# Six steps of an attention kernel form their own numerators by features, in four column tiles, and turn them back by DMA

## The chip, the cores and the metric

The kernel runs on one core of a Trainium2 chip. Its time is the device time of one execution, in microseconds (us), and the median over a few runs is what is compared. One further execution was recorded by the hardware profiler; its span (first to last instruction) and its own time are given below. The engines are PE (matrix products; PEld is its weight load), DVE (vector), ACT (scalar, exponentials), POOL (GpSimd) and SP (which here only issues DMAs).

## What is computed

Two attention layers over the same 2048 tokens of width 640 (32 heads of 20 features), mixed by a gate. Layer A is linear attention with softmax feature maps. Layer B, where the change lies, goes over the tokens in four segments of 512. Within a segment it is causal softmax attention, between segments a memory is carried:

```python
for s in range(4):                      # segments of L = 512 tokens
    p = softmax(qs @ ks.T * scale + mask)           # per head, causal
    a_dot = p @ vs                                  # "own" numerators over their denominators
    num, den = phi(qs) @ M, phi(qs) @ z + 1e-6      # the memory of earlier segments
    o = g * num / den + (1 - g) * a_dot
    M, z = M + phi(ks).T @ vs, z + phi(ks).sum(...)
return gate * A(x) + (1 - gate) * (concat(o) @ wo)
```

## The kernel before, in words

The first 126 us prepare weights, run layer A and the projections of B's first segment. From about 126.9 us on B's attention runs; the program is written out by hand there, engine by engine, in the order in which the Python code emits it.

**Steps and double steps.** A step is one segment and one group of four heads, so there are 4 x 8 = 32 (`Step`, L735); step k belongs to segment k // 8. Two steps a and b make a double step, of which there are 16, numbered 0 to 15. A double step has five bursts (`bursts`, L771). A burst (`emit_burst`, L751) writes scores of four heads into two PSUM tiles `st_ps` (L757, four row groups of PE, one for each head), ACT takes the exponential of each tile into `PT` (L761, 128 x 1024, key tokens on the partitions and query tokens along the columns), and POOL zeroes the triangles of the diagonal blocks (L768). The two tiles come from two pools of one buffer each, so PE can write a tile of the next burst only when ACT has read the one before.

**Own numerators.** `pv_items` (L805) makes, for each 128-query block j and head i, a sum over the key blocks c <= j: the weights are a 128 x 128 block of `PT`, the moving operand is `vB`, 20 value features and a column of ones, so that the denominator comes as column 21. That is 4 x (1 + 2 + 3 + 4) = 40 matmuls of 21 columns for a step (L811), with query tokens on the PSUM partitions. They go to bank 0 of `nda`, of which there is one. `mem_items` (L815) adds four matmuls with the memory (L819) and, except in the last segment, four that add to it (L824), in bank 1.

**Epilogue.** `emit_epi` (L831): DVE takes the reciprocal of both kinds of denominators (L836), multiplies it by the gates (L838) and both kinds of numerators by that (L848); POOL adds the two into `oB` (L851). For segments before the last, DVE and POOL also update the memory (L854, L857, L858).

**Fillers.** Between the bursts PE does dense work from a list: `h`, half projections for the next segment (L943), `o` and `f`, halves of output rows (L887; `f` of an early chunk is ten matmuls of 320 columns, otherwise five). All of it uses `proj` PSUM tiles, two buffers in all, and DVE moves each result out (L949, L898, L896). `t` issues on SP the DMA transpose of an `oB` chunk (`emit_oT`, L860, at L862), `u` the last four such (L981). SP is one queue and also carries the row outputs (L900).

**The order.** For each double step `PLAN` (L971) is a string: `A` and `D` are the first and last part of the own numerators of step a, with `D` also the memory's; `B` and `C` the same for the step b of the double step before; the other letters are fillers and feature work. Every item has a planned price, and `SHARES` (L976) says what part of the sum of prices is emitted before each of the five bursts.

Of the kernel before, what the change touches and what calls it, by code (L numbers as in the profile page):

```python
# [15 lines left out]
def kernel(  # L16
# [16 lines left out]
    P = 128  # L33
# [421 lines left out]
    kv_stack.close()  # L455
    a3_stack = ExitStack()
    resB = ctx.enter_context(tc.tile_pool(name="resB", bufs=1))
    vBs = [resB.tile([P, 4, H, DH + 1], BF16, name=f"vB{n}") for n in range(2)]
    a3e = a3_stack.enter_context(tc.tile_pool(name="a3e", bufs=KC, side="right", reuse_waits="tile"))
    a3w = a3_stack.enter_context(tc.tile_pool(name="a3w", bufs=2, side="right", reuse_waits="tile"))  # L460
    for W, src in ((WkB, B_wk), (WqB, B_wq)):
# [107 lines left out]
    def emit_zsum():  # L569
        emit_zz(emit_z(z_den[:, 0]))  # L570
        open_stages()
        for vB in vBs:
            nc.gpsimd.memset(vB[:, :, :, DH:DH + 1], 1.0)

    def emit_first_den():
        for n in range(NB):
# [130 lines left out]
    with ExitStack() as bctx:  # L707
# [24 lines left out]

        GP = 4 * (DH + 1)

        class Step:  # L735
            def __init__(self, k):
                self.s, self.g = divmod(k, G)
                self.PT = {}
                self.last = k == NSEG * G - 1
                self.nda = nda  # L740
                if self.g == 0:
                    oBs[self.s] = bw.tile([P, 4, D], BF16, name="oB")
                    og = Eqf[:, 2 * G * L + 2 * L + (self.s % 2) * L:2 * G * L + 2 * L + (self.s % 2 + 1) * L]
                    og = og.bitcast(F32).rearrange("p (n j h) -> p n j h", n=2, j=4)
                    om = omgS[:, 4 * self.s:4 * self.s + 4, None].to_broadcast([P, 4, H])
                    nc.gpsimd.tensor_tensor(out=og[:, 0], in0=om, in1=omgh_b[:, None, :].to_broadcast([P, 4, H]),
                                            op=ALU.mult)
                    nc.gpsimd.tensor_copy(out=og[:, 1], in_=om)
                    ogs[self.s] = og
# [55 lines left out]
        def pv_items(st, js):  # L805
# [6 lines left out]
                                     rhs=vB[:, c, 4 * st.g + i, :], start=(c == 0), stop=(c == j))  # L812
            return [(0.026 * (j + 1), lambda j=j, i=i: piece(j, i)) for j in js for i in range(4)]

        def mem_items(st):  # L815
            g = st.g

            def am(j):
                nc.tensor.matmul(st.nda[:, 1, j * GP:(j + 1) * GP], lhsT=phiq_block(st.s, g, j),  # L819
                                 rhs=Mbd[:, g].rearrange("p i e -> p (i e)"), start=True, stop=True)  # L820

            def mz(c):
                Mz = st.nda[:, 1, 4 * GP:5 * GP].rearrange("p (i e) -> p i e", i=4)
                nc.tensor.matmul(Mz, lhsT=phiks[st.s % 2][:, c, 4 * g:4 * g + 4, :],  # L824
                                 rhs=vBs[st.s % 2][:, c, 4 * g:4 * g + 4, :],
                                 start=(c == 0), stop=(c == 3))
            return ([(0.037, lambda j=j: am(j)) for j in range(4) if st.s > 0]
                    + [(0.037, lambda c=c: mz(c)) for c in range(4) if st.s < NSEG - 1]
                    + [(0.0, lambda: emit_epi(st))])

        def emit_epi(st):  # L831
            s, g = st.s, st.g
            n = 2 if s > 0 else 1
            ndv = st.nda[:, 0:n, 0:4 * GP].rearrange("p n (ji e) -> p n ji e", e=DH + 1)
            rec = bw.tile([P, 2, 16], F32, name="rec")
            nc.vector.reciprocal(out=rec[:, 0:n], in_=ndv[:, :, :, DH])  # L836
            recv = rec[:, 0:n].rearrange("p n (j i) -> p n j i", j=4)
            nc.vector.tensor_tensor(out=recv, in0=recv,  # L838
                                    in1=ogs[s][:, 0:n, :, 4 * g:4 * g + 4],
                                    op=ALU.mult)  # L840
            rb = rec[:, 0:n, :, None].to_broadcast([P, n, 16, DH])
            oview = oBs[s][:, :, g * 80:(g + 1) * 80].rearrange("p j (i d) -> p j i d", d=DH)
            if n == 1:
                nc.vector.tensor_tensor(out=oview, in0=ndv[:, 0, :, 0:DH].rearrange("p (j i) d -> p j i d", j=4),
                                        in1=rb[:, 0].rearrange("p (j i) d -> p j i d", j=4), op=ALU.mult)
            else:
                td = bw.tile([P, 2, 16, DH], F32, name="td")
                nc.vector.tensor_tensor(out=td, in0=ndv[:, :, :, 0:DH], in1=rb, op=ALU.mult)  # L848
                tdv = td.rearrange("p n (j i) d -> p n j i d", j=4)
                eng = nc.vector if s == NSEG - 1 and g == G - 2 else nc.gpsimd  # L850
                eng.tensor_tensor(out=oview, in0=tdv[:, 0], in1=tdv[:, 1], op=ALU.add)  # L851
            if s < NSEG - 1:
# [81 lines left out]
        def run_first(fns):  # L934
            if fns:
                fns.pop(0)()

        def half_item(part, sc, half):
            W = {"k": WkB, "q": WqB, "v": WvB}[part]
            hs = slice(half * 16, (half + 1) * 16)  # L940

            def mm(ps, k):
                nc.tensor.matmul(ps, lhsT=xq[:, sc // 4, k, sc % 4 * P:(sc % 4 + 1) * P],  # L943
                                 rhs=W[:, k, half * 320:(half + 1) * 320],
                                 start=(k == 0), stop=(k == KC - 1))
# [22 lines left out]

        PLAN = ("qhhhyzhokxooAD", "qhhByhChkzoxAooD", "qhhByhChkzxoAooD",  # L971
                "ooBqoyokCozxoADo", "hkhBhhChhqhyAhDztt", "khhBxhhqChfhyzAD",
                "khhBxhhqCfyzADt", "khhBxhhqChfyhzAD", "khhxtBhhqChyhADzt",
                "hhBhhqChfyhzAD", "hhBhhqCfhyzAthD", "hhBhhqhCftyhzAD",
                "fBftCfftAD", "ffBtCfftAD", "fBtfCffADf", "fBCuffAffD")
        SHARES = [[0.2, 0.42, 0.55, 0.78], [0.19, 0.4, 0.6, 0.84], [0.2, 0.4, 0.6, 0.81], [0.19, 0.38, 0.59, 0.78], [0.19, 0.38, 0.58, 0.81], [0.18, 0.41, 0.65, 0.86], [0.2, 0.4, 0.6, 0.83], [0.19, 0.4, 0.6, 0.83], [0.2, 0.4, 0.6, 0.8], [0.22, 0.39, 0.6, 0.82], [0.19, 0.39, 0.61, 0.82], [0.2, 0.39, 0.6, 0.82], [0.2, 0.4, 0.6, 0.8], [0.21, 0.4, 0.61, 0.8], [0.19, 0.37, 0.59, 0.82], [0.2, 0.41, 0.6, 0.84]]  # L976

        oT4 = oTA[:, 0:4]

# [7 lines left out]
        for dstep in range(NSEG * G // 2):  # L987
# [5 lines left out]
            for w in PLAN[dstep]:  # L993
                if w in "hfo":
                    items += {"h": halves, "f": fins, "o": aouts}[w].pop(0)
                elif w in "xy":
                    items.append((0.0, lambda part="kq"[w == "y"]: run_first(sums[part])))
                elif w in "kq":
                    items.append((0.0, lambda part=w: run_first(waiting[part])))
                elif w == "z":  # L1000
                    items.append((0.0, lambda: run_first(q_turns)))
                elif w == "u":
                    items += [(0.0, lambda n=n: turn_last(n)) for n in range(4)]
                elif w == "t":
                    items.append((0.0, lambda ch=turns.pop(0): emit_oT(ch)))
                else:
                    st = a if w in "AD" else prev
                    items += pv_items(st, (0, 1, 2)) if w in "AB" else pv_items(st, (3,)) + mem_items(st)
            whole = sum(w for w, _ in items)
            done = 0.0  # L1010
            for n, burst in enumerate(bursts(a, b)):
# [159 lines left out]
```

## Time and profile before

| | us |
|---|---|
| median of 3 runs | 316.44 (316.29 to 316.65) |
| the profiled execution, its own time | 315.58 |
| its span, first to last instruction | 313.6 |
| first exponential of double step 0 | 126.88 |
| first exponential of double steps 11, 12, 13, 14, 15 | 248.13, 259.41, 270.80, 281.16, 291.96 |
| end of the last exponential | 302.89 |

So 2.0 us of the execution lie outside the span, and the profiled execution is 0.86 us faster than the median. The first exponential of a double step is the tenth, twentieth and so on of the 160 instructions of L761 in the trace; their distance is used below as the length of a double step: 11.28, 11.39, 10.36, 10.80 and 10.93 us for 11 to 15.

In a row of the profile's timeline stand the start, the time from the first to the last instruction of a group, the engine, line, operation, operands, count and, in brackets, the idle time before it. PE rows overlap, since a matmul's recorded end lies behind the start of the next: what a group costs PE is the distance from its start to the next group's start.

### The profile page before, as it was taken

Reading aid. Unit: us, or ns where it says so; the run is one execution under the profiler, and the core shown is the slowest. Engines: PE = TensorE matmul, PEld = TensorE weight load, DVE = VectorE, ACT = ScalarE, POOL = GpSimd, SP = SyncE. Lnnn points to the kernel's source line nnn. Section 1 sums busy time; section 2 is a strip of 40 time slices with the busy share of each in tenths; the row PEclk is TensorE's granted clock in tenths of the full one; section 3 lists DMA queues with packets and bytes.
Section 4 is the critical chain, followed back from the end, with each engine's and each line's share of the span. In section 5 each row is a group of like instructions: output and inputs, shape, how many; then the busy total and the mean of one; then the engine's idle time right before and its main releaser. Section 6 shows DMA issues by size and latency. Waiting matters only on the chain.

```text
span 313.6 us, 10096 instructions
## 1 busy us (share of the span) xinstructions
PE 303.6 (97%) x4182; PEld 208.4 (66%) x4182; DVE 224.0 (71%) x508; ACT 252.0 (80%) x320; POOL 206.8 (66%) x308
## 2 busy tenths in 40 slices
PE   8999999999999999999999999999999999999995
PEld 7788877755578778465666666565666666565673
DVE  3477997999779997677758588777755765455553
ACT  4677888267846648999998999999998898998953
POOL 8588599103247989955657577688786877666550
PEclk9999999999999999999999999999999999999999
DMA  7989944439217998775421394473745545222132
GB/s 216 199 184 204 210 108 129 127 89 365 74 36 106 130 136 147 135 100 99 55 50 36 69 127 86 59 120 69 110 84 78 86 100 72 64 78 53 48 90 84
DMA packets 94007, 34.56 MB, mean 110 GB/s; under 512 B 82442, under 2 KB 93834, under 8 KB 93962
## 3 DMA queue, kind: packets, MB, share of 16 engines
q1 hardware_dynamic: 93386, 33.28, 54.4%
q10 hardware_dynamic: 576, 0.66, 0.7%
q8 instruction: 32, 0.52, 0.7%
q14 instruction: 13, 0.11, 0.1%
HBM read 6.10 MB, written 2.62 MB: 28 GB/s over the span
## 4 chain that ended last, share of the span: by engine, by line
PE 69%; ACT 19%; DVE 4%; POOL 3%; issue 2%; DMA 1%; ACTq 0%; DVEq 0%; POOLq 0%
ACT PT L761 16%; PE proj L943 10%; PE st_ps L757 10%; PE proj L887 9%; PE pk L242 7%; PE pq L420 7%; PE nda L811 7%; PE pv L242 7%; PE proj L557 3%; PE num L478 2%; PE kv_ps L393 2%; DVE tt L527 1%; DMA oTA<-oA 1%; POOL oA L686 1%; DVE rr L503 1%
## 5 line engine op out<-in xcount | busy, mean ns | idle before, releaser
L761 ACT ACTIVATE PT<-st_ps 128x1024 bf16<-128x1024 f32 x160 | 153.9, 1023 | 12.2 <-PE st_ps L757 9.8
L768 POOL TENSOR_SCALAR_AFFINE_SELECT PT<-PT 128x512 bf16<-128x512 bf16 (+1 forms) x130 | 84.4, 668 | 46.7 <-ACT PT L761 46.3
L811 PEld LDWEIGHTS <-PT 128*128 128x128 bf16 x1280 | 40.0, 96 | 9.0 <-issue 5.4
L811 PE MATMUL nda<-vB,PT 128*128 128x21 bf16 x1240 | 41.5, 173 | 0.1
L261 POOL TENSOR_TENSOR EkSn<-Ek,krec 128x1280 bf16<-128x1280 bf16 x15 | 35.1, 2360 | 9.2 <-DVE krec L260 7.3
L943 PEld LDWEIGHTS <-xTf 128*128 128x128 bf16 x300 | 26.5, 97 | 13.8 <-issue 5.3
L949 DVE CAST Z<-proj 128x320 bf16<-128x320 f32 x44 | 21.1, 488 | 16.7 <-PE proj L943 15.6
L427 ACT ACTIVATE Eq<-pq 128x1024 bf16<-128x1024 f32 x20 | 19.4, 1021 | 12.2 <-PE pq L420 12.2
L257 DVE TENSOR_REDUCE ksum<-Ek 128x64 f32<-128x1280 bf16 x16 | 23.6, 1474 | 7.2 <-ACT Ek L253 7.2
L527 DVE TENSOR_TENSOR tt<-num,rr 128x640 f32<-128x640 f32 x32 | 25.0, 812 | 4.6 <-POOL rr L520 1.8
L686 POOL TENSOR_TENSOR oA<-tt 128x640 bf16<-128x640 f32 x16 | 24.6, 1545 | 5.3 <-DVE tt L527 5.0
L887 PE MATMUL proj<-WkA,oTA 128*128 128x320 bf16 x160 | 28.0, 300 | 0.0
L757 PE MATMUL st_ps<-Z 32*128 32x512 bf16 (+3 forms) x256 | 24.9, 299 | 3.0 <-ACT PT L761 2.5
L253 ACT ACTIVATE Ek<-pk 128x640 bf16<-128x640 f32 x32 | 20.8, 703 | 7.9 <-PE pk L242 6.8
L757 PE MATMUL st_ps<-Eq 32*128 32x512 bf16 (+3 forms) x256 | 25.2, 299 | 1.5 <-ACT PT L761 1.2
L242 PEld LDWEIGHTS <-xTf 128*128 128x128 bf16 x200 | 22.6, 113 | 4.7
L851 POOL TENSOR_TENSOR oB<-td 128x320 bf16<-128x320 f32 x22 | 19.6, 889 | 4.4 <-DVE td L848 3.6
L420 PE MATMUL pq<-xTf,WqA 128*128 128x512 bf16 x100 | 22.4, 379 | 0.0
L887 PE MATMUL proj<-WvA,oT 128*128 128x320 bf16 x120 | 21.3, 300 | 0.0
L848 DVE TENSOR_TENSOR td<-nda,rec 128x640 f32<-128x640 f32 x23 | 19.0, 825 | 2.5 <-DVE rec L838 0.5
L836 DVE RECIPROCAL rec<-nda 128x32 f32<-128x32 f32 (+1 forms) x31 | 10.3, 331 | 12.8 <-PE nda L824 8.1
L887 PEld LDWEIGHTS <-oTA 128*128 128x128 bf16 x160 | 13.6, 97 | 8.3 <-issue 4.2
(183 smaller groups left out, 558.8 us busy)
## 6 DMA issues: line engine op xcount, KB each, us to landing
Z<-EkSn SPq DMA_DIRECT2D x32, 160.0 KB, 2.8
out_dram<-orow SPq DMA_DIRECT2D x8, 160.0 KB, 1.9
out_dram<-oTA SPq DMA_DIRECT2D x6, 160.0 KB, 1.8
WvA<-in_A_wqkv_dram SPq DMA_DIRECT2D x2, 400.0 KB, 6.4
WvB<-in_B_wv_dram SPq DMA_DIRECT2D x1, 800.0 KB, 4.7
WkB<-in_B_wk_dram SPq DMA_DIRECT2D x1, 800.0 KB, 6.5
WqB<-in_B_wq_dram SPq DMA_DIRECT2D x1, 800.0 KB, 8.2
WkA<-in_A_wo_dram SPq DMA_DIRECT2D x1, 800.0 KB, 11.3
```

Of the source, the lines that this page charges most:

```text
L242: nc.tensor.matmul(ps[:, bk, 0:n], lhsT=key_tokens(c, sc), rhs=rhs, start=(c == 0), stop=(c == by_row[-1][0] if sc == 0 and W is WkA else ...
L257: nc.vector.tensor_reduce(out=ksum, in_=Ek.rearrange("p s (h f) -> p (s h) f", f=DH), axis=AX.X, op=ALU.add)
L261: (nc.vector if sc == NCH - 1 else nc.gpsimd).tensor_tensor(out=EkSn[:, sc].rearrange("p s (h f) -> p (s h) f", f=DH), in0=Ek.rearrange("p ...
L420: nc.tensor.matmul(pq[:, half, :], lhsT=WqA[:, c, j * P:(j + 1) * P], rhs=xq[:, 2 * qb + half, c], start=(c == 0), stop=(c == KC - 1))
L527: nc.vector.tensor_tensor(out=tt[:, sgn].rearrange("p (b h) d -> p b h d", b=2), in0=ps, in1=csb, op=ALU.mult)
L686: nc.gpsimd.tensor_tensor(out=oA.rearrange("p (h d) -> p h d", d=DH), in0=tt[:, 0], in1=tt[:, 1], op=ALU.add)
L757: nc.tensor.matmul(ps[:, i - i0, o:o + L - c * P], lhsT=kT[32 * i:32 * i + 32, c * P:(c + 1) * P], rhs=qT[32 * i:32 * i + 32, c * P:L], st ...
L761: nc.scalar.activation(out=PT[:, i0:i0 + 2], in_=ps, func=ACT.Exp, scale=SCALE_B)
L768: nc.gpsimd.affine_select(out=v, in_=v, pattern=[[0, n_i], [1, P]], compare_op=ALU.is_ge, fill=0.0, base=0, channel_multiplier=-1)
L811: nc.tensor.matmul(nd[:, j, i], lhsT=block(st, c)[:, i, (j - c) * P:(j - c + 1) * P], rhs=vB[:, c, 4 * st.g + i, :], start=(c == 0), stop= ...
L887: nc.tensor.matmul(ps, lhsT=oT[:, k % KC], rhs=W[:, k % KC, hs], start=(k == 0), stop=(k == n - 1))
L943: nc.tensor.matmul(ps, lhsT=xq[:, sc // 4, k, sc % 4 * P:(sc % 4 + 1) * P], rhs=W[:, k, half * 320:(half + 1) * 320], start=(k == 0), stop ...
```

## The change

Six steps, 22 and 24 to 28, are "turned". (22 is step a of double step 11; 24, 26, 28 are steps a of 12, 13, 14; 25 and 27 are steps b of 12 and 13 and so worked on as `B` in 13 and 14.) In them the value features are the weights, 32 columns of `vB` (21 used, 11 that belong to what lies behind them), and the exponentials are the moving operand. Head i goes to column tile i of PE, so to PSUM partitions 32i and on; each of the four key blocks gives four matmuls, one for each head, of 512, 384, 128 and 256 columns: 16 in all. Features then stand on the partitions and tokens along the columns. DVE copies that bank as bf16 to `LT`, SP issues a DMA transpose of it to `LN`, and the own half of the epilogue (`fin`) is put off: it is emitted after the next turned step's, or ahead of the `B` or `A` of the next step that isn't turned. `LT` has two places, taken in turn: a tile of its own and `zt`, which is free by then; `LN` has two buffers. The memory's matmuls come ahead of the 16, and all stands where `A` or `B` stood; `D` and `C` are empty in these steps. The memory's half of the epilogue follows the copy.

`vB` gets 12 zero columns behind it (two more memsets), so that 32 columns can be read for the last head. And the strings of all double steps but 2 and 7 are changed, with some shares: letters move within their double step, except that one `t` goes from double step 6 to 5.

```diff
+        TURNED = {22, 24, 25, 26, 27, 28}
+        fins_due = []
+        LTs = [None, zt.rearrange("p c t -> p (c t)")[:, 0:L]]
...
+        def turned_items(st):
+            def mm():
+                for c in (0, 1, 3, 2):
+                    for i in range(4):
+                        o = (c * H + 4 * st.g + i) * (DH + 1)
+                        nc.tensor.matmul(st.nda[32 * i:32 * i + 32, 0, c * P:L], lhsT=vBf[st.s % 2][:, o:o + 32],
+                                         rhs=block(st, c)[:, i, 0:L - c * P], start=(c == 0), stop=(c == 2),
+                                         tile_position=(0, 32 * i))
+                LTs.append(LTs.pop(0))
+                LT = LTs[-1] if LTs[-1] is not None else bw.tile([P, L], BF16, name="LT", bufs=1)
+                nc.vector.tensor_copy(out=LT, in_=st.nda[:, 0])
+                st.LN = bw.tile([P, 4, P], BF16, name="LN", bufs=2)
+                nc.sync.dma_start_transpose(out=st.LN, in_=LT)
+                emit_epi_turned(st)
+                run_fins(1)
+            return mem_items(st)[:-1] + [(0.73, mm)]
+
+        def emit_epi_turned(st):
...
+            def scale(n, den, v, eng):
+                recv = rec[:, n].rearrange("p (j i) -> p j i", j=4)
+                nc.vector.reciprocal(out=recv, in_=den)
+                nc.vector.tensor_tensor(out=recv, in0=recv, in1=og[:, n, :, 4 * g:4 * g + 4], op=ALU.mult)
+                eng.tensor_tensor(out=td[:, n].rearrange("p (j i) d -> p j i d", j=4), in0=v,
+                                  in1=recv[:, :, :, None].to_broadcast([P, 4, 4, DH]), op=ALU.mult)
...
+            scale(1, mv[:, :, :, DH], mv[:, :, :, 0:DH], nc.vector)
+
+            def fin():
+                lv = st.LN.rearrange("p j (i e) -> p j i e", i=4)
+                scale(0, lv[:, :, :, DH], lv[:, :, :, 0:DH], nc.vector)
+                tdv = td.rearrange("p n (j i) d -> p n j i d", j=4)
+                nc.gpsimd.tensor_tensor(out=oBs[s][:, :, g * 80:(g + 1) * 80].rearrange("p j (i d) -> p j i d", d=DH),
+                                        in0=tdv[:, 0], in1=tdv[:, 1], op=ALU.add)
+            fins_due.append(fin)
+            emit_state(st)
...
+        def run_fins(keep=0):
+            while len(fins_due) > keep:
+                fins_due.pop(0)()
...
-        PLAN = ("qhhhyzhokxooAD", "qhhByhChkzoxAooD", "qhhByhChkzxoAooD",
-                "ooBqoyokCozxoADo", "hkhBhhChhqhyAhDztt", "khhBxhhqChfhyzAD",
-                "khhBxhhqCfyzADt", "khhBxhhqChfyhzAD", "khhxtBhhqChyhADzt",
-                "hhBhhqChfyhzAD", "hhBhhqCfhyzAthD", "hhBhhqhCftyhzAD",
-                "fBftCfftAD", "ffBtCfftAD", "fBtfCffADf", "fBCuffAffD")
+        PLAN = ("qhhhyzhokxoAoD", "qhhByhChkzoAoxoD", "qhhByhChkzxoAooD",
+                "ooBqoyokCozoxADo", "hhBkhhChhqhyAhzDtt", "khhBxhhqChtfhyzAD",
+                "khhBxhhqCfyzAD", "khhBxhhqChfyhzAD", "khhxtBhhqChyhAzDt",
+                "hhBhhqChfhyzAD", "hhBhhqCfhyhzAtD", "hhBhhqhCfthyzAD",
+                "ffBtCfftAD", "ffBtCffADt", "fBtCfffADf", "fBCufffAfD")
...
-                    items += pv_items(st, (0, 1, 2)) if w in "AB" else pv_items(st, (3,)) + mem_items(st)
+                    if st.turned:
+                        items += turned_items(st) if w in "AB" else []
+                    else:
+                        items += ([(0.0, run_fins)] + pv_items(st, (0, 1, 2)) if w in "AB"
+                                  else pv_items(st, (3,)) + mem_items(st))
```

More of the change, by code (lines that the diff above doesn't have):

```diff
@@ L457 @@
     resB = ctx.enter_context(tc.tile_pool(name="resB", bufs=1))
-    vBs = [resB.tile([P, 4, H, DH + 1], BF16, name=f"vB{n}") for n in range(2)]
+    VW = 4 * H * (DH + 1)
+    vBf = [resB.tile([P, VW + 12], BF16, name=f"vB{n}") for n in range(2)]
+    vBs = [t[:, 0:VW].rearrange("p (c h e) -> p c h e", c=4, h=H) for t in vBf]
     a3e = a3_stack.enter_context(tc.tile_pool(name="a3e", bufs=KC, side="right", reuse_waits="tile"))
@@ L571, in emit_zsum @@
         open_stages()
-        for vB in vBs:
+        for vB, vf in zip(vBs, vBf):
             nc.gpsimd.memset(vB[:, :, :, DH:DH + 1], 1.0)
+            nc.gpsimd.memset(vf[:, VW:VW + 12], 0.0)
     def emit_first_den():
@@ L739, in __init__ @@
                 self.last = k == NSEG * G - 1
+                self.turned = k in TURNED
                 self.nda = nda
@@ new lines, in emit_epi_turned @@
+        def emit_epi_turned(st):
+            s, g = st.s, st.g
+            mv = st.nda[:, 1, 0:4 * GP].rearrange("p (ji e) -> p ji e", e=DH + 1)
+            rec = bw.tile([P, 2, 16], F32, name="rec")
+            td = bw.tile([P, 2, 16, DH], F32, name="td")
+            og = ogs[s]
+            def scale(n, den, v, eng):
[4 more added lines that the diff above has]
+                                  in1=recv[:, :, :, None].to_broadcast([P, 4, 4, DH]), op=ALU.mult)
+            mv = st.nda[:, 1, 0:4 * GP].rearrange("p (j i e) -> p j i e", j=4, i=4)
+            scale(1, mv[:, :, :, DH], mv[:, :, :, 0:DH], nc.vector)
[7 more added lines that the diff above has]
+            emit_state(st)
@@ L851, in emit_epi, with emit_state @@
                 eng.tensor_tensor(out=oview, in0=tdv[:, 0], in1=tdv[:, 1], op=ALU.add)
+            emit_state(st)
+        def emit_state(st):
+            s, g = st.s, st.g
             if s < NSEG - 1:
@@ L966 @@
         turns = [0, 1, 2, 3, 4, 5, 6, 7, 10, 8, 9, 11]
-        PLAN = ("qhhhyzhokxooAD", "qhhByhChkzoxAooD", "qhhByhChkzxoAooD",
-                "ooBqoyokCozxoADo", "hkhBhhChhqhyAhDztt", "khhBxhhqChfhyzAD",
-                "khhBxhhqCfyzADt", "khhBxhhqChfyhzAD", "khhxtBhhqChyhADzt",
-                "hhBhhqChfyhzAD", "hhBhhqCfhyzAthD", "hhBhhqhCftyhzAD",
-                "fBftCfftAD", "ffBtCfftAD", "fBtfCffADf", "fBCuffAffD")
-        SHARES = [[0.2, 0.42, 0.55, 0.78], [0.19, 0.4, 0.6, 0.84], [0.2, 0.4, 0.6, 0.81], [0.19, 0.38, 0.59, 0.78], [0.19, 0.38, 0.58, 0.81], [0.18, 0.41, 0.65, 0.86], [0.2, 0.4, 0.6, 0.83], [0.19, 0.4, 0.6, 0.83], [0.2, 0.4, 0.6, 0.8], [0.22, 0.39, 0.6, 0.82], [0.19, 0.39, 0.61, 0.82], [0.2, 0.39, 0.6, 0.82], [0.2, 0.4, 0.6, 0.8], [0.21, 0.4, 0.61, 0.8], [0.19, 0.37, 0.59, 0.82], [0.2, 0.41, 0.6, 0.84]]
+        PLAN = ("qhhhyzhokxoAoD", "qhhByhChkzoAoxoD", "qhhByhChkzxoAooD",
[3 more added lines that the diff above has]
+                "ffBtCfftAD", "ffBtCffADt", "fBtCfffADf", "fBCufffAfD")
+        SHARES = [[0.2, 0.42, 0.54, 0.79], [0.19, 0.4, 0.6, 0.84], [0.2, 0.4, 0.6, 0.81], [0.19, 0.38, 0.59, 0.78], [0.19, 0.39, 0.58, 0.81], [0.18, 0.41, 0.65, 0.86], [0.2, 0.4, 0.6, 0.83], [0.18, 0.4, 0.6, 0.84], [0.2, 0.42, 0.6, 0.8], [0.22, 0.39, 0.6, 0.82], [0.19, 0.39, 0.61, 0.82], [0.2, 0.39, 0.6, 0.82], [0.19, 0.41, 0.6, 0.8], [0.19, 0.4, 0.6, 0.77], [0.19, 0.39, 0.58, 0.82], [0.2, 0.41, 0.6, 0.84]]
         oT4 = oTA[:, 0:4]
```

## The prediction

> **What bounds the kernel now.** I read the page's totals first, then the busy times by double step, then PE's and DVE's rows in time.
>
> ```profile
> span 313.6 us, 10096 instructions
> ...
> PE 303.6 (97%) x4182; PEld 208.4 (66%) x4182; DVE 224.0 (71%) x508; ACT 252.0 (80%) x320; POOL 206.8 (66%) x308
> ```
>
> PE's 97% is no proof of a full PE, since a waiting matmul counts. So I price PE's work in the double steps that hold the turned steps. The busy times in double steps 11 to 15:
>
> ```profile
> core 0: us, PE busy (x) PEld busy (x) DVE busy (x) ACT busy (x) POOL busy (x), PEclk, DMA share, GB/s
> 248.13:259.41 11.28, 11.28 (x170) 7.39 (x168) 7.88 (x17) 10.24 (x11) 8.12 (x15) 1.00 0.78 109
> 259.41:270.80 11.39, 11.36 (x167) 7.19 (x166) 5.36 (x12) 9.69 (x11) 8.49 (x17) 1.00 0.27 62
> 270.80:281.16 10.36, 10.15 (x152) 6.08 (x150) 5.10 (x10) 9.69 (x11) 6.30 (x11) 1.00 0.26 65
> 281.16:291.96 10.80, 10.55 (x155) 6.38 (x154) 5.74 (x12) 9.62 (x11) 6.52 (x10) 1.00 0.29 74
> 291.96:302.89 10.93, 10.69 (x159) 7.04 (x159) 5.22 (x12) 9.66 (x11) 7.28 (x12) 1.00 0.27 67
> ```
>
> The reader is to see ACT at 9.6 to 10.2 us in each, whatever the length, and DVE half idle from 259 us on. Prices for PE come from its timeline:
>
> ```profile
> 275.20 1.16 PE L811 MATMUL nda<-vB,PT 128*128 128x21 bf16 x40
> 276.21 0.31 PE L819 MATMUL nda<-Mbd,xTf 128*128 128x84 bf16 x4
> 276.46 0.80 PE L757 MATMUL st_ps<-Eq 32*128 32x512 bf16 x4
> 277.19 0.31 PE L887 MATMUL proj<-WvA,oT 128*128 128x320 bf16 x1
> ```
>
> Start to start, the 40 own matmuls take 1.01 us, 25 ns each. Five dense matmuls of 320 columns take 0.69 us in a row (266.20 to 266.89), 0.1375 each, 0.43 ns a column. Four L819 take 0.15 us ahead of a matmul of their own kind (290.54 to 290.69) but 0.25 ahead of a burst here, so passing between whole-array and row-tiled matmuls costs 0.10. The cleanest burst takes 0.44 us with both passings (261.29 to 261.73). With these, PE needs in double step 12: 40 dense 5.50 + 80 own 2.02 + 12 small 0.45 + five bursts 2.2 = 10.2 us, more than ACT's 9.7. In 13: 30 dense 4.12 + 2.02 + 0.30 + 2.2 = 8.6, less than ACT. In 14: 35 dense 4.81, so 9.3 against 9.6. In 11: 10.3 against 10.2. Yet all four are 0.7 to 1.2 us longer than the larger of the two. The loss is in the handover: PE comes late to some bursts (ACT idles 0.2 to 0.5 us, released by L757) and early to others (PE waits in the burst: the L757 group above takes 0.73 us where 254.56 to 254.89 shows 0.33 for the same four). So less PE work helps fully where PE is the longer, and partly elsewhere.
>
> **PE's part of the change.** Removed for a step: 40 x 25 ns = 1.01 us. Added: 16 matmuls in four column tiles. No row shows four, but the key-value sums of layer A show two, 64 columns wide with 80 columns moving:
>
> ```profile
> core 0: us, PE busy (x) PEld busy (x), PEclk, DMA share, GB/s
> 57.15:61.00 3.85, 3.85 (x190) 3.61 (x189) 1.00 0.59 167
> ```
>
> That is 20.3 ns a matmul, where 80 columns alone would take 34: two run beside each other. If four do, each key block costs its columns once: 512, 384 and 256 at 0.43 are 0.50 us; the 128-column block is held at 4 x 20.3 = 0.08 by the pace of the row; with two passings at 0.10 the sum is 0.78 us. Bounds: 0.58 with both passings shared with a burst; 1.30 + 0.20 = 1.50 if only two streams run (16 x 320 columns at the row's 80 per 20.3 ns). I take 0.78, since the row is one of full overlap paced by issue: 20.3 ns is below the 25 of the L811 pair. It saves 0.23 a step, 0.5 in a double step with two.
>
> What reaches the end: in 12 PE is the longer, so 0.24. In 11 PE and ACT are level: half, 0.12. In 13 ACT is the longer and only 0.67 us lie above it: half of 0.48, 0.24. In 14 there are 1.18 us above ACT: three quarters, 0.36. These shares are chosen, between none and all (0 to 1.4). Together 0.96 us. No double step gains where no step is turned.
>
> **A wait that goes.** Bank 0 of the single `nda` is now free after a copy, not after reciprocal, multiply and product. Before, this is met once in the stretch: eight dense matmuls from 287.61 end at 288.71, the own matmuls start at 288.96, just behind DVE's product (0.82 us from 288.09).
>
> ```profile
> 287.61 1.26 PE L887 MATMUL proj<-WvA,oT 128*128 128x320 bf16 x8
> 288.96 0.68 PE L811 MATMUL nda<-vB,PT 128*128 128x21 bf16 x21
> ```
>
> I take 0.24 gained (0 to 0.25); late next would be DVE's copy itself.
>
> **DVE's part.** An epilogue before:
>
> ```profile
> 276.56 0.36 DVE L836 RECIPROCAL rec<-nda 128x32 f32<-128x32 f32 x1 [0.67 <-PE nda L819]
> 276.95 0.60 DVE L838 TENSOR_TENSOR rec<-rec,Eq 128x32 f32<-128x32 f32 x1
> 277.66 0.82 DVE L848 TENSOR_TENSOR td<-nda,rec 128x640 f32<-128x640 f32 x1
> 278.40 0.48 DVE L896 TENSOR_TENSOR oTA<-proj,oTA 128x320 bf16<-128x320 f32 x1
> ```
>
> By means 0.36 + 0.32 + 0.83 = 1.50 us. After: a copy of 128x512, 0.68 (L898's 0.49 for 320 and 1.0 ns for each of 192 more, from 320 against 640 in L1054 and L848); the memory's half, by the 16- and 320-wide rows, 0.26 + 0.21 + 0.49 = 0.95; `fin` the same 0.95 from SBUF. In all 2.6, so 1.1 more a step. With two steps in 13 and 14 DVE goes from 5.1 and 5.7 to some 7.3 and 7.9 us of 10: it fits as a sum. What it delays is the evictions queued behind: with copy, half and an older `fin` in a row, DVE is taken for 2.7 us. In 14, after `B`, PE has ten dense matmuls, five more and one or two bursts (2.5 to 2.9 us) before it needs the buffer whose eviction DVE reaches at 2.7 and ends at 3.2. I take 0.2 lost in all (0 to 0.5 at each of the five turned steps in 12 to 14).
>
> L838 takes 0.17 to 0.61 us for the same small shape, both inputs in SBUF. `fin` has three such operations where the old epilogue had one. The Trainium skill (SBUF — State Buffer, section "SBUF: two separate sides") says that such a DVE operation and a GpSimd operation that reads SBUF exclude each other for a whole instruction; the spread of L838 agrees. By it a `fin` would lose up to 3 x 0.4 = 1.2 us, which belongs to the rival on DVE below.
>
> **SP and its waits.** Each turned step adds a transpose on SP, waiting for the copy; behind it stand row outputs and `t`. The nearest rows:
>
> ```profile
> L862 SPq DMA_TRANSPOSE oT<-oB x12: 1199/1258/2256, 183.4 to 286.5; - x12
> ...
> DMA to landing us min/median/max: 2.6/2.7/4.1
> ```
>
> With 0.68 for the copy `LN` lands some 3.5 us after the matmuls (up to 4.8, or behind a blocked `t` more). `fin` comes a later turned step on, at 3 to 5 us, after that step's copy and half, another 1.6: hidden. `fin` of 22 stands behind two outputs in 12 and ahead of a `B` that doesn't need it; that of 28 comes behind some 4 us of DVE work. The four `u` transposes need step 28's sum; I put them 2 us later than now (294.23), with the first needed at 302.25 (L1067) and landing by 300: hidden.
>
> **At nothing:** the two memsets (POOL idles 7.40 us behind them); POOL's additions (same count); the memory's matmuls (moved, not added). The other orders: they take no work away. Double steps 1 and 2, near alike in their strings, differ by 0.27 us in length (10.83 and 11.10), so ten changed ones may move the end by some 0.9 either way; I take 0.
>
> **Sum:** -0.96 - 0.24 + 0.2 = -1.0 us. The profiled execution's 315.58 becomes 314.6; on the median, 0.86 higher, 316.44 becomes **315.4**. Its own range is 314.2 to 315.8. About 0.2%, 0.63 us, is what a measurement here can tell from no change.
>
> **Rivals.**
> - *The handover keeps the time* (0.23): ACT's 9.7 us and the burst-to-burst wait set the double steps, and PE's saving turns into PE waiting in L757. For it: PE already waits there in 13. Against: ACT idles for PE ahead of most bursts of 12 and 14. Time 316.4, within 0.3.
> - *DVE becomes late* (0.13), slower. Place: evictions of `proj` and the reads of `nda` behind copy, half and `fin`. If `fin` meets POOL each time, DVE is taken for 2.7 + 1.2 = 3.9 us, against 2.9 that two buffers bridge: 1.0 lost at each of the two steps `B` and near 0.5 at the three `A`, 3.5 in all, less the 1.2 gained: 318.7; at half of that 317.0. It decides once an eviction comes later than PE's third dense half. Against: DVE idles 1 to 3 us at a time for L887 now. The Trainium skill (TensorEngine Tiling (Array Packing), "PSUM Bottleneck") says that tiling speeds PE but not the emptying of PSUM, which may become the bound. By that rule this rival would be the outcome.
> - *Column tiles share their streams* (0.09), slower: 1.50 - 1.01 = 0.5 us more a step, six times, 2.9 us: 319.3. For it: each head brings a moving operand of all 128 partitions, where four row tiles share them. Against: the two-tile row.
>
> **Chances:** forecast 0.55, then 0.23, 0.13 and 0.09. So faster 0.55, the same 0.23, slower 0.22. The range 313.8 to 317.6 takes all of PE's saving with luck of the orders at its low end, and half of the DVE rival at its high end; it leaves out the streams and the worst of DVE, and some 0.07 below.
>
> **What would show it.** Right: 16 matmuls in 0.7 to 0.8 us start to start; double steps 13 and 14 each 0.2 to 0.4 us shorter, 0 to 10 unmoved in sum. Wrong: a block over 1.0 us; DVE's `fin` idle for `LN`; dense matmuls or L819 waiting for DVE; double steps 0 to 10 moving by over 0.9 us, which would be the orders, not the tiles.

## The result, and the profile after

The changed kernel takes 314.36 us (median of 22 runs, 313.38 to 315.94), the kernel before 315.46 in 22 runs on the same chip (314.28 to 316.76). The ratio is 0.9955, with a 95% interval of 0.9942 to 0.9969: faster by 1.42 us, 1.0 to 1.8 (the two medians alone lie 1.10 apart). The profiled execution took 314.34 us with a span of 312.6; its last exponential ends at 302.05. In the changed kernel L773 is the exponential, L769 the scores, L832 the turned matmuls, L837 the copy, L839 the transpose to `LN`, L854 to L856 the scaling, L866 the POOL addition of `fin`, L875 the memory's matmuls, L894 the old epilogue's second operation and L947 the output rows.

The changed kernel's totals, from its page:

```profile
span 312.6 us, 9844 instructions
...
PE 302.4 (97%) x4038; PEld 204.9 (66%) x4038; DVE 230.4 (74%) x532; ACT 251.9 (81%) x320; POOL 205.5 (66%) x310
```

PE has 144 matmuls fewer (six times 40 - 16), DVE 6.4 us more: 1.07 us for each turned step. Its busy times in double steps 11 to 15, with the columns as before:

```profile
core 0: us, PE busy (x) PEld busy (x) DVE busy (x) ACT busy (x) POOL busy (x), PEclk, DMA share, GB/s
248.09:259.26 11.17, 11.08 (x146) 6.78 (x144) 6.96 (x16) 10.30 (x11) 7.70 (x14) 1.00 0.68 106
259.26:270.36 11.10, 11.10 (x142) 6.61 (x140) 7.21 (x18) 9.70 (x11) 8.68 (x18) 1.00 0.49 75
270.36:280.44 10.08, 9.43 (x104) 4.78 (x102) 6.11 (x16) 9.53 (x10) 5.60 (x10) 1.00 0.40 93
280.44:290.85 10.41, 10.12 (x107) 5.10 (x106) 7.44 (x21) 9.68 (x10) 6.51 (x11) 1.00 0.43 104
290.85:302.05 11.20, 11.03 (x160) 7.24 (x160) 7.74 (x18) 9.70 (x11) 8.08 (x13) 1.00 0.24 49
```

The first number after each window is its length. Four of the five are shorter, and 13 comes nearest to ACT's own time (0.55 us above it); 15, in which only the left-over work of step 28 is turned, is longer. Double steps 0 to 10 take 121.18 us, where they took 121.25. A turned block in PE's timeline (start, time from first to last, count at the end):

```profile
268.96 0.32 PE L875 MATMUL nda<-Mbd,xTf 128*128 128x84 bf16 x4
269.21 0.73 PE L832 MATMUL nda<-PT,vB 128*32 128x512 bf16 x16
269.87 0.64 PE L769 MATMUL st_ps<-Eq 32*128 32x512 bf16 x4
```

From start to next start the 16 matmuls take 0.66 us, the four ahead of them 0.25. The other five blocks take 0.66 as well.

### The profile page after: what moved, and what is told of

Its sections match the earlier page's. It is cut to its first block, busy times and chain, and to the rows that moved or that the text cites. A ratio compares the mean times of both kernels' runs of the same rounds, so it can differ in the third digit from the quotient of the medians.

```text
span 312.6 us, 9844 instructions
## 1 busy us (share of the span) xinstructions
PE 302.4 (97%) x4038; PEld 204.9 (66%) x4038; DVE 230.4 (74%) x532; ACT 251.9 (81%) x320; POOL 205.5 (66%) x310
## 4 chain that ended last, share of the span: by engine, by line
PE 68%; ACT 21%; DVE 5%; POOL 3%; issue 2%; ACTq 0%; DVEq 0%; POOLq 0%
ACT PT L773 18%; PE proj L1007 10%; PE st_ps L769 9%; PE proj L947 8%; PE pk L242 7%; PE pq L420 7%; PE pv L242 7%; PE nda L823 5%; PE proj L560 3%; DVE tt L530 2%; PE num L481 2%; PE kv_ps L393 2%; DVE rr L506 2%; POOL oA L690 1%; PE warm L318 1%
## 5 line engine op out<-in xcount | busy, mean ns | idle before, releaser
L773 ACT ACTIVATE PT<-st_ps 128x1024 bf16<-128x1024 f32 x160 | 153.9, 1024 | 11.4 <-PE st_ps L769 9.3
L823 PEld LDWEIGHTS <-PT 128*128 128x128 bf16 x1040 | 32.9, 96 | 7.8 <-issue 4.5
L1007 PEld LDWEIGHTS <-xTf 128*128 128x128 bf16 x300 | 26.5, 97 | 14.1 <-issue 5.5
L823 PE MATMUL nda<-vB,PT 128*128 128x21 bf16 x1000 | 34.2, 173 | 0.0
L947 PE MATMUL proj<-WkA,oTA 128*128 128x320 bf16 x160 | 28.3, 300 | 0.0
L769 PE MATMUL st_ps<-Z 32*128 32x512 bf16 (+3 forms) x256 | 25.2, 299 | 3.0 <-ACT PT L773 2.5
L769 PE MATMUL st_ps<-Eq 32*128 32x384 bf16 (+3 forms) x256 | 25.6, 299 | 1.9 <-ACT PT L773 1.5
L242 PEld LDWEIGHTS <-xTf 128*128 128x128 bf16 x200 | 22.6, 113 | 4.7
L947 PE MATMUL proj<-WvA,oT 128*128 128x320 bf16 x120 | 21.2, 300 | 0.0
L947 PEld LDWEIGHTS <-oTA 128*128 128x128 bf16 x160 | 13.5, 97 | 8.6 <-issue 4.6
L560 PEld LDWEIGHTS <-xTf 128*128 128x128 bf16 x180 | 15.8, 97 | 4.6
L769 PEld LDWEIGHTS <-Z 32*128 32x128 bf16 x256 | 7.5, 91 | 16.2 <-issue 15.0
L481 PEld LDWEIGHTS <-Eq 128*128 128x128 bf16 x320 | 15.9, 96 | 3.3 <-issue 0.7
```

What stands on the lines that cost most here:

```text
L242: nc.tensor.matmul(ps[:, bk, 0:n], lhsT=key_tokens(c, sc), rhs=rhs, start=(c == 0), stop=(c == by_row[-1][0] if sc == 0 and W is WkA else ...
L560: nc.tensor.matmul(ps, lhsT=xq[:, sc // 4, cc, sc % 4 * P:(sc % 4 + 1) * P], rhs=W[:, cc, half * 320:(half + 1) * 320], start=(cc == 0), s ...
L769: nc.tensor.matmul(ps[:, i - i0, o:o + L - c * P], lhsT=kT[32 * i:32 * i + 32, c * P:(c + 1) * P], rhs=qT[32 * i:32 * i + 32, c * P:L], st ...
L773: nc.scalar.activation(out=PT[:, i0:i0 + 2], in_=ps, func=ACT.Exp, scale=SCALE_B)
L823: nc.tensor.matmul(nd[:, j, i], lhsT=block(st, c)[:, i, (j - c) * P:(j - c + 1) * P], rhs=vB[:, c, 4 * st.g + i, :], start=(c == 0), stop= ...
L947: nc.tensor.matmul(ps, lhsT=oT[:, k % KC], rhs=W[:, k % KC, hs], start=(k == 0), stop=(k == n - 1))
```

## The experiments

Twelve kernels ran in three groups, each group on one chip with the kernel before beside it; the change had run in a group of its own. Between groups ratios agree to about 0.2% only (e10, whose double steps add up to those of the change, reads 0.9978 beside 0.9955), so the lengths of the double steps in each profiled execution are the finer measure: in the changed kernel and e3, which differ in one DVE operand, 11 to 14 agree within 0.01 us each. All of them (the sums are added before rounding):

| | 11 | 12 | 13 | 14 | 15 | sum | median, us | ratio to before (95%) |
|---|---|---|---|---|---|---|---|---|
| before | 11.28 | 11.39 | 10.36 | 10.80 | 10.94 | 54.76 | | |
| the change | 11.17 | 11.10 | 10.09 | 10.41 | 11.20 | 53.96 | 314.36 | 0.9955 (0.9942 to 0.9969) |
| e1_orders_alone | 11.37 | 11.14 | 10.68 | 10.64 | 10.94 | 54.78 | 315.43 | 0.9994 (0.9981 to 1.0007) |
| e2_turned_alone | 11.07 | 12.07 | 9.95 | 10.81 | 11.69 | 55.59 | 315.97 | 1.0012 (0.9996 to 1.0028) |
| e3_fin_no_wait | 11.16 | 11.09 | 10.09 | 10.40 | 10.93 | 53.68 | 313.99 | 0.9946 (0.9928 to 0.9963) |
| e4_one_block | 10.87 | 10.92 | 9.79 | 10.38 | 10.93 | 52.88 | 313.43 | 0.9931 (0.9912 to 0.9950) |
| e5_fin_after_epilogue | 11.16 | 11.09 | 10.09 | 10.41 | 11.40 | 54.16 | 314.77 | 0.9979 (0.9967 to 0.9992) |
| e6_turned_23_too | 11.16 | 10.77 | 10.45 | 10.31 | 11.51 | 54.20 | 314.80 | 0.9978 (0.9962 to 0.9993) |
| e7_two_copies | 11.16 | 11.09 | 10.09 | 10.96 | 11.29 | 54.60 | 314.96 | 0.9983 (0.9971 to 0.9995) |
| e8_old_orders_no_wait | 11.08 | 12.07 | 9.95 | 10.81 | 11.12 | 55.04 | 315.49 | 1.0003 (0.9984 to 1.0022) |
| e9_old_orders_new_12 | 11.07 | 11.12 | 10.02 | 10.74 | 11.81 | 54.76 | 314.97 | 0.9987 (0.9973 to 1.0001) |
| e10_a28_earlier | 11.16 | 11.09 | 10.09 | 10.64 | 10.98 | 53.96 | 314.58 | 0.9978 (0.9966 to 0.9991) |
| e11_head_by_head | 11.19 | 11.10 | 10.15 | 10.38 | 11.31 | 54.12 | 314.68 | 0.9981 (0.9963 to 0.9999) |
| e12_23_and_a28 | 11.16 | 10.76 | 10.45 | 10.64 | 10.99 | 53.99 | 314.45 | 0.9971 (0.9954 to 0.9987) |

### The two halves of the change: orders alone, turning alone

```diff
-        TURNED = {22, 24, 25, 26, 27, 28}
+        TURNED = set()
```

> No step is turned; the strings and shares of the changed kernel stay. Theory T (the turned steps' PE time is the gain): within 0.3 us of the kernel before, ratio 0.999 to 1.001, double steps 0 to 10 unmoved. Rival O (the orders are the gain): 1 us or more faster, ratio 0.997 or less.

The other half keeps the turned steps and has `PLAN` and `SHARES` of before:

> The six steps are turned, with the strings and shares of before. Theory T: 0.7 to 1.2 us faster than before (ratio 0.996 to 0.998), less by what the unfitted order loses in double steps 13 to 15. Rival O: no faster than before, 1.000 or more.

Neither half gains: e1's sum is that of before within 0.02 us (12 shorter by 0.25, 13 longer by 0.32), as theory T had it; e2's is 0.83 us longer, against theory T. Only both together give -0.80. So the new orders are worth 1.63 us (55.59 to 53.96) once steps are turned, and nothing without. In e2 double step 12 is the place: 12.07 us. Its PE timeline, with the idle time ahead of a group in brackets:

```profile
260.05 0.84 PE L947 MATMUL proj<-WvA,oT 128*128 128x320 bf16 x5
261.64 0.30 PE L823 MATMUL nda<-vB,PT 128*128 128x21 bf16 x6 [0.74 <-DVE mtmp L914]
```

and what DVE does meanwhile:

```profile
259.42 0.67 DVE L837 CAST LT<-nda 128x512 bf16<-128x512 f32 x1
260.01 0.24 DVE L854 RECIPROCAL rec<-nda 128x16 f32<-128x16 f32 x1
260.29 0.55 DVE L855 TENSOR_TENSOR rec<-rec,Eq 128x16 f32<-128x16 f32 x1
260.94 0.49 DVE L856 TENSOR_TENSOR td<-nda,rec 128x320 f32<-128x320 f32 x1
261.35 0.23 DVE L914 TENSOR_TENSOR mtmp<-nda,CM 128x84 f32<-128x84 f32 x1
```

The own matmuls of the next step are not released by the copy, which is done by 260.1, but by the last reader of the whole `nda` (L914, which reads the memory's bank), 1.5 us later. The string of e2 has one `f` ahead of `B`; its ten dense matmuls cover only half of that. The new one, `ffBtCfftAD`, has two.

### One string of the new orders

```diff
-                "fBftCfftAD", "ffBtCfftAD", "fBtfCffADf", "fBCuffAffD")
+                "ffBtCfftAD", "ffBtCfftAD", "fBtfCffADf", "fBCuffAffD")
```

This is e2 with that string, and the new shares, for double step 12 alone.

> The six steps turned with the old strings and shares, except that double step 12 has its new string (two f instead of one ahead of B) and shares. If what the old string lost there was PE waiting 0.74 us ahead of B for DVE to let go of nda (its copy and the memory's half, 1.6 us): double step 12 falls from 12.07 to 11.1 to 11.2, the others stay (9.95, 10.81, 11.69), and the time is 0.9 us below that of the old orders throughout. If the loss was made elsewhere: 12 stays above 11.7.

12 falls from 12.07 to 11.12 us, 0.95. That is about what the release of `nda` had cost: in e2 0.90 us from start to start, beyond the pace of a dense matmul (the 0.74 in brackets counts from a modelled end). In e9 PE doesn't wait there. The sum gains 0.83 of the 1.63; of the 0.81 left, 0.61 stands in 15 (11.81) and 0.33 in 14, while 11 and 13 are a little shorter than in the change.

### The wait for the transpose

```diff
-                lv = st.LN.rearrange("p j (i e) -> p j i e", i=4)
+                lv = vBf[s % 2][:, 0:4 * P].rearrange("p (j t) -> p j t", j=4).rearrange("p j (i e) -> p j i e", i=4)
```

> The put-off half reads value columns that lie ready in place of LN (so the own half of six steps is not computed from the numerators); copy and transposes stay. If DVE's waits for LN (1.6 us in double step 12, 1.2 in 15) cost the end nothing: as the changed kernel, within 0.2 us. If the wait in 15 is what lengthened that double step by 0.26 us: 0.2 to 0.4 us faster than the changed kernel, and double step 15 back to 10.9.

15 falls to 10.93 us, the length it had before the change, and 11 to 14 stay. So the wait costs 0.27 us, all of it in 15. It begins on SP, where the transpose of step 28 is issued at

```profile
290.42 1.20 SPq L839 DMA_TRANSPOSE LN<-zt  x1
```

DVE in the changed kernel:

```profile
292.89 0.48 DVE L958 CAST orow<-proj 128x320 bf16<-128x320 f32 x1
294.52 0.25 DVE L854 RECIPROCAL rec<-LN 128x16 f32<-128x16 bf16 x1 [1.15 <-DMA LN<-zt]
294.81 0.17 DVE L855 TENSOR_TENSOR rec<-rec,Eq 128x16 f32<-128x16 f32 x1
295.02 0.49 DVE L856 TENSOR_TENSOR td<-LN,rec 128x320 f32<-128x320 bf16 x1
```

and POOL behind it:

```profile
295.60 0.86 POOL L866 TENSOR_TENSOR oB<-td 128x320 bf16<-128x320 f32 x1 [1.49 <-DVE td L856]
296.41 1.22 POOL L780 TENSOR_SCALAR_AFFINE_SELECT PT<-PT 128x512 bf16<-128x512 bf16 x2
297.60 0.86 POOL L907 TENSOR_TENSOR oB<-td 128x320 bf16<-128x320 f32 x1
298.41 1.82 POOL L780 TENSOR_SCALAR_AFFINE_SELECT PT<-PT 128x512 bf16<-128x512 bf16 x3
```

The reader is to see a chain through three engines: `LN` lands 4.1 us after its issue, DVE's `fin` idles 1.15 us for it, POOL's addition is late by that, and the triangles that PE's own matmuls of step 30 need stand behind the additions in POOL's queue. PE's rows show where it ends. The first 24 own matmuls of step 30, and what follows them, in the changed kernel:

```profile
298.56 0.96 PE L823 MATMUL nda<-vB,PT 128*128 128x21 bf16 x24
299.37 0.30 PE L947 MATMUL proj<-WvA,oT 128*128 128x320 bf16 x1
```

and in e3:

```profile
299.92 0.76 PE L823 MATMUL nda<-vB,PT 128*128 128x21 bf16 x24
300.53 0.30 PE L947 MATMUL proj<-WvA,oT 128*128 128x320 bf16 x1
```

From start to next start they take 0.81 us against 0.61: in the changed kernel the fifteenth waits until 299.10, when POOL's first triangle of the last row above is done. That is 0.20 of the 0.27. The other 0.07 lies in the dense matmuls ahead of them, where PE waits for an eviction that DVE, late by `fin`, reaches only at 297.35. In 12 the same wait for `LN` is longer (1.63 us), and the length of 12 does not change without it: nothing behind it there was needed so soon.

The same edit under the old orders tells whether that wait made e2 slow:

> The six steps turned with the strings and shares of before, and the put-off half reading value columns that lie ready in place of LN (the own half of six steps is not computed). If the old orders lost only by DVE waiting for LN in front of evictions: double step 12 falls from 12.07 to 11.0 to 11.2, 15 from 11.69 to 11.0 to 11.3, and the time to 0.8 to 1.3 us below the kernel before. If the orders matter for PE's bursts: 12 stays above 11.5.

12 stays at 12.07, only 15 falls (11.69 to 11.12). So the loss in 12 is not the transpose (e9 showed it to be the release of `nda`), and of the 0.75 us that 15 had lost in e2, 0.57 is. In e2 PE waits for POOL's triangles outright, in the middle of the same 24 matmuls:

```profile
300.04 0.41 PE L823 MATMUL nda<-vB,PT 128*128 128x21 bf16 x10 [0.59 <-POOL PT L780]
```

### Two ways of moving that wait

`fin` behind the next step's epilogue:

```diff
-                        items += ([(0.0, run_fins)] + pv_items(st, (0, 1, 2)) if w in "AB"
-                                  else pv_items(st, (3,)) + mem_items(st))
+                        items += (pv_items(st, (0, 1, 2)) if w in "AB"
+                                  else pv_items(st, (3,)) + mem_items(st) + [(0.0, run_fins)])
```

> The put-off halves of steps 22 and 28 are emitted behind the next unturned step's epilogue instead of ahead of its own matmuls, so that DVE does that epilogue first. If DVE's waits for LN cost what the run without the wait showed: double step 15 back from 11.20 to 10.9, double step 12 within 0.1, in all 0.2 to 0.3 us faster than the changed kernel, ratio to before 0.994 to 0.995. Rival: the wait only moves to the next DVE work, as the changed kernel.

This made 15 longer, 11.40. POOL in that kernel:

```profile
295.50 1.23 POOL L780 TENSOR_SCALAR_AFFINE_SELECT PT<-PT 128x512 bf16<-128x512 bf16 x2 [1.22 <-ACT PT L773]
296.69 0.86 POOL L907 TENSOR_TENSOR oB<-td 128x320 bf16<-128x320 f32 x1
297.97 0.86 POOL L866 TENSOR_TENSOR oB<-td 128x320 bf16<-128x320 f32 x1 [0.43 <-DVE td L856]
298.79 1.82 POOL L780 TENSOR_SCALAR_AFFINE_SELECT PT<-PT 128x512 bf16<-128x512 bf16 x3
```

DVE's wait is gone, but `fin`'s addition now stands directly ahead of the last triangles and holds them back to 298.79, 0.2 later than in the changed kernel when counted from the first exponential of 15. DVE is late as well: its product in this `fin` takes 1.11 us instead of 0.49, and an eviction behind it holds PE up:

```profile
298.35 0.84 PE L947 MATMUL proj<-WvA,oT 128*128 128x320 bf16 x5 [0.20 <-DVE oTA L956]
```

The triangles are the wait that ends last: the own matmuls, begun late by that eviction, still stop for them. So the order of both queues, DVE's and POOL's, matters here. The other way issues the transpose earlier, by an `A` ahead of an `f` in double step 14:

```diff
-                "ffBtCfftAD", "ffBtCffADt", "fBtCfffADf", "fBCufffAfD")
+                "ffBtCfftAD", "ffBtCffADt", "fBtCffAfDf", "fBCufffAfD")
```

> The changed kernel with step 28's block one f earlier in double step 14, so that LN of 28 lands some 0.7 us earlier. If the wait for it, and POOL's addition behind it, made double step 15 longer: 15 at 10.95 to 11.05 instead of 11.20, 14 within 0.1, in all 0.1 to 0.25 us faster. Rival: 14 grows by what 15 wins, since the block now comes between other bursts.

15 gains 0.22 and 14 loses 0.23, as the rival had it: the sum is unmoved (53.96).

### What the matmuls themselves are worth

```diff
-                for c in (0, 1, 3, 2):
+                for c in (0,):
...
-                                         rhs=block(st, c)[:, i, 0:L - c * P], start=(c == 0), stop=(c == 2),
+                                         rhs=block(st, c)[:, i, 0:L - c * P], start=True, stop=True,
```

> Of the 16 matmuls of a turned step only the four of the first key block are left (12 left out, the own numerators are incomplete): PE's block shrinks by some 0.35 us. By the shares of the prediction (half in double steps 11 and 13, all in 12, three quarters in 14) 1.4 us faster than the changed kernel. Rival H (the handover keeps the time, PE is no longer the bound there): 0.4 or less.

A block now takes 0.33 us from start to start, so 0.33 a step is gone: once in 11 and in 12, twice, so 0.65, in 13 and in 14. Against the changed kernel the double steps lose 0.30, 0.18, 0.30, 0.03 and 0.27: 1.08 us in all, between the two forecasts. PE's time goes through nearly whole in 11, by half in 12 and 13 and hardly at all in 14, where nothing tried got below 10.3. The 0.27 of 15, which has no turned matmuls, is the wait for `LN` again; this kernel's trace has none there. In 14 PE now waits for ACT ahead of tiles of two bursts, 0.34 and 0.50 us, where the trace of the changed kernel lists no such wait: the handover between PE and ACT takes up what is saved. What would shorten 14 was not found.

One step more, 23, the `B` of double step 12, turned (on top of e5):

```diff
-        TURNED = {22, 24, 25, 26, 27, 28}
+        TURNED = {22, 23, 24, 25, 26, 27, 28}
...
-                "ffBtCfftAD", "ffBtCffADt", "fBtCfffADf", "fBCufffAfD")
+                "ffBtCffADt", "ffBtCffADt", "fBtCfffADf", "fBCufffAfD")
```

> The same, with step 23 turned as well (worked on as B in double step 12, where PE's work is the longer) and the second t of that double step moved behind A. Theory T: double step 12 shorter by 0.1 to 0.25 us (0.18 of 0.35 us came through there when 12 matmuls were left out), the rest as before it. Rival D (DVE late): double step 12 longer, by DVE's 1.1 us more in a double step that already holds two such chains.

Against e5, 12 gains 0.32 and 13 loses 0.36: the gain is more than expected and does not reach the end. The same with `A` of step 28 earlier and `fin` where the change has it:

> The changed kernel with step 23 turned too (its t behind A) and step 28's block one f earlier; the put-off halves where the change has them. Double step 12 at 10.8, as with step 23 turned before; 15 at 11.0; 13 at 10.1 to 10.5. If 13 keeps 10.1: 0.3 to 0.5 us faster than the changed kernel. If 13 goes to 10.45 as it did with 23 turned before: no faster.

13 goes to 10.45, and the sum is 53.99, the changed kernel's within 0.03. No version that computes the whole result beats the change by more than the measurement can tell.

### DVE's margin

```diff
                 nc.vector.tensor_copy(out=LT, in_=st.nda[:, 0])
+                nc.vector.tensor_copy(out=LT, in_=st.nda[:, 0])
```

> The changed kernel with the copy of each turned step made twice, 0.69 us more of DVE in each of six steps. Theory T (DVE has slack, evictions are rarely late): 0 to 0.4 us slower than the changed kernel. Rival D (DVE is at its limit): 1 us or more slower.

14 grows by 0.55 us, 15 by 0.10, 11 to 13 not at all, though 12 holds one added copy and 13 two, as 14 does. The 0.65 in all lies between what the two theories expected. PE in that kernel, in 14:

```profile
287.09 0.72 PE L948 MATMUL proj<-WvA,oT 128*128 128x320 bf16 x4
288.30 0.84 PE L948 MATMUL proj<-WvA,oT 128*128 128x320 bf16 x5 [0.50 <-DVE orow L959]
```

PE waits 0.50 us for an eviction (L959, L958 in the changed kernel): the third half of output rows behind `B` needs the buffer that DVE has not emptied. In the changed kernel that wait is not there: the eviction ends 0.4 us ahead of the matmul that needs its buffer. So DVE's cover in 14 is less than one copy, 0.69 us; in 12 and 13 the added copies delay nothing.

### The order of the sixteen

```diff
-                for c in (0, 1, 3, 2):
-                    for i in range(4):
+                for i in range(4):
+                    for c in (0, 1, 3, 2):
```

> The same 16 matmuls, the four of one head (one column tile) behind each other instead of the four heads of one key block. If tiles overlap only with what stands next to them in PE's queue: the block grows from 0.66 to 1.8 to 2.2 us, six times, and the kernel is 5 to 8 us slower than the changed one. Rival: PE takes matmuls of idle tiles ahead of waiting ones, the block stays near 0.7 and the time too.

PE's timeline:

```profile
268.81 0.32 PE L875 MATMUL nda<-Mbd,xTf 128*128 128x84 bf16 x4
269.06 0.76 PE L832 MATMUL nda<-PT,vB 128*32 128x512 bf16 x16
269.75 0.64 PE L769 MATMUL st_ps<-Eq 32*128 32x512 bf16 x4
```

0.69 us instead of 0.66: the order hardly matters. What I expected of it fell; more below. Its double steps are within 0.12 us of the changed kernel's, and its ratio reads 0.9981: that is the 0.2% between groups.

## Why the prediction was right, step by step

**The sign, and the size at the end, came out; the way there only in part.** Forecast -1.0 us, measured -1.42 (1.0 to 1.8); in the two profiled executions -0.80 in double steps 11 to 15, -0.04 ahead of them and some -0.4 behind the last exponential (0.13) and outside the span (0.27), for which I had no term and have no cause. The runs show the second part too: what a run takes beyond its span is 1.7 to 1.8 us in all 136 runs of kernels with turned steps, while in the 95 runs of the kernel before whose spans are on record it goes up to 3.4 and is 1.94 on average; e1, which turns nothing, looks like before.

So the size is partly luck: in the double steps less came than forecast, and the rest came from places that the sum did not hold. The time itself, 315.4, missed by 1.0 us, since the 316.44 that I started from was the median of only three runs; 22 gave 315.46. e10, with the change's sum, gained 0.7 us in its group, so 1.42 lies at the upper end of what these runs show.

- **PE's block: right in size, its saving too small.** 0.66 us and 0.10 for the passing ahead of it (0.25 for the four L875 where 0.15 is their pace) against 0.78. In the trace the four 512-column matmuls start at 0, 4, 7 and 10 ns, the 384s at 226, the 128s at 389 and the 256s at 444: each key block costs its columns once, even the short one, which takes 55 ns where I held it at 81. With that the rival of shared streams (1.50 us) is out. But the old block had a passing of 0.10 ahead of a burst too, which I left out of the sum. Four of the six blocks stand ahead of a burst: there 1.01 + 0.25 became 0.25 + 0.66, a saving of 0.35 us instead of 0.23. With 0.25 or more for the other two it is some 1.9 us in all, where I had 1.4.
- **What reaches the end: the total near, the places wrong.** I put -0.12, -0.24, -0.24 and, with the wait of `nda`, -0.60 on 11 to 14; before to after shows -0.11, -0.29, -0.27, -0.39. That agreement is partly chance. Against e1, which has the same orders without the turning, turning gives -0.20, -0.04, -0.59, -0.23 and +0.26. The -0.29 of 12 is the orders' own (-0.25 in e1), and so is a loss in 13 (+0.32 in e1) that the two blocks there more than make up. In 11 to 14 together turning gives some 1.1 of the 1.9 us: my shares were too high, the saving that they were taken from too low, and the two errors offset each other.
- **Orders at nothing: wrong as it was put.** I wrote that they take no work away and may move the end by 0.9 either way. Alone they move it by 0.0; with the turned steps by 1.63. They are a condition of the gain: in 12, half of that, since they put dense work where `nda` is held (e9); how the other half, in 14 and 15, comes about was not taken apart.
- **"A wait that goes": wrong in its reason.** Bank 0 is not free after the copy. `nda` is let go as a whole, after copy and memory's half, 0.69 + 0.25 + 0.17 to 0.55 + 0.49 = 1.6 us and more, where the old epilogue took 1.50. The wait that I had found, 0.25 us in 14, is in none of the traces of e1, e2 and the change, so it went with either half and not by an earlier release; in its place the old orders have one of 0.74 us in 12 (e2).
- **`LN` hidden: wrong in 15.** It landed 4.8 us behind the matmuls, the most that I had allowed, but `fin` of 28 comes behind only 3.0 us of DVE work (290.39 to 293.37), not 4. `fin` idle for `LN` was a sign of being wrong that I had named, and it came, in 12 (without cost) and in 15. There it cost 0.27 us (e3), of which 0.20 by way of POOL's queue, which the working had not followed, and 0.07 by a late eviction.
- **DVE: right, with little to spare.** Copy 0.69 (0.68 predicted), 1.07 us more a step (1.1). A `fin` mostly takes 0.24 + 0.17 + 0.49 = 0.90. Nothing was lost to late evictions in 11 to 14, where I had put 0.2; in 15 it was 0.07. The rival needed more DVE work than there is, but e7 shows its mechanism, at the place named (14, third half behind `B`), less than one copy of 0.69 us away. The Trainium skill (TensorEngine Tiling (Array Packing), "PSUM Bottleneck") warns that emptying PSUM may become the bound: no such bound in the change, 0.55 us of it in e7. By the Trainium skill (SBUF — State Buffer, "SBUF: two separate sides") I had allowed 1.2 us lost in each `fin` to POOL, for three operations; only two of them have two inputs in SBUF, since the reciprocal reads one. In the trace of the change a product of `fin` takes 0.49 and at most 0.81 us, 0.32 more, and that one runs beside POOL's triangles; in e5 one takes 1.11.
- **The handover rival** (0.23) holds for 14, where e4 takes 0.65 us off PE and 0.03 reach the end. In e6, e10 and e12 each gain in one double step went in a neighbour, which fits it. In 13 it holds by half (0.30 of 0.65), in 11 not (0.30 of 0.33).

## What to carry to other kernels

A shorter block on a full engine is worth what the order of the work around it lets through: measure order and block apart and together, since here neither half gained alone. In this kernel a tile of two banks is let go as a whole, by its last reader, so moving one bank out early freed nothing; two tiles in its place were not tried. And a wait that is hidden on the engine that waits may still be paid by a third engine whose queue is behind it.

## What the runs showed of the hardware that I had not expected

**PE starts matmuls of idle column tiles ahead of earlier ones.** In e11 the program has all four matmuls of head 0, then those of head 1, and so on. In the trace the four 512-column ones, one of each head, start at 0, 14, 27 and 40 ns, and head 0's second at 226. The trace does not number the instructions, but their spacing fits that order: 13 to 14 ns is four times the 3 to 4 ns between the same four in the changed kernel, where they follow each other directly. So the program's order is kept within a column tile, not between them. The Trainium skill (TensorE: Matmul & The Clock Gate, Part 3, "The mechanism") says that matmuls start and end strictly in program order; this measurement differs, and it decides.

**The granted clock can fall for a few microseconds on one core.** In the profiled execution of e3 (windows, the clock is the third number from the end):

```profile
core 0: us, PE busy (x) PEld busy (x) DVE busy (x) ACT busy (x) POOL busy (x), PEclk, DMA share, GB/s
200.00:203.00 3.00, 3.00 (x62) 1.98 (x61) 2.53 (x6) 2.79 (x4) 1.84 (x2) 1.00 0.15 55
203.00:206.00 3.00, 2.79 (x14) 1.51 (x12) 1.99 (x5) 2.74 (x4) 2.94 (x7) 0.64 0.49 93
206.00:209.00 3.00, 3.00 (x47) 1.79 (x45) 2.24 (x4) 1.94 (x2) 1.00 (x3) 0.79 0.35 66
```

Its ten dense matmuls there:

```profile
203.61 2.68 PE L1007 MATMUL proj<-WqB,xTf 128*128 128x320 bf16 x10
```

and the same ten in the changed kernel:

```profile
203.57 1.53 PE L1007 MATMUL proj<-WqB,xTf 128*128 128x320 bf16 x10
```

Double step 7 takes 12.66 us there instead of 11.27, 1.4 more; e4's profiled execution shows the same (0.59 and 0.84). In a window cut to it, 203.83 to 207.24, e3's clock is 0.50: half speed for 3.4 us, though PE was busy for 3.2 of the 3.4 us ahead of it. That is why the lengths of 0 to 10, and the ends, of these two are not compared. What sets it off stays open. It isn't what spreads the times: in all 22 runs of the changed kernel the mean clock is 0.999 or 1.000, and they spread over 2.6 us.
